# Three more weight slots, two more x tiles turned on the matmul engine, and score banks lent out at the end: a change to a fused attention and gated feed-forward kernel

## The chip, the cores and the metric

The kernel runs on one core of one Trainium2 chip. The metric is the device time of one execution in microseconds (us); the times quoted are medians of several executions. "PE" is the matmul engine (TensorE), "PEld" its weight load, "DVE" the vector engine, "ACT" the scalar engine, "POOL" GpSimd and "SP" the engine that issues most DMAs. Each execution also reports the span from its first to its last instruction and the mean clock that the throttle granted PE, as a share of full speed.

A ratio between two kernels is the mean time of one kernel's runs over the mean of the other's of the same rounds, so it is not quite the ratio of the medians beside it. Intervals are 95%.

## The reference, cut to what matters

```python
def _A_ref(x, wq, wk, wv, wo):            # x: (1, 2048, 1024), bf16
    q = (x @ wq).reshape(B, S, 32, 32).transpose(0, 2, 1, 3)     # 32 heads of 32
    k, v = x @ wk, x @ wv                                        # one key and value head for all
    p = softmax(einsum("bhqd,bkd->bhqk", q, k) * 32 ** -0.5)
    o = einsum("bhqk,bkd->bhqd", p, v)
    return o.transpose(0, 2, 1, 3).reshape(B, S, 1024) @ wo
def _B_ref(x, w_gate, w_up, w_down):      # 1024 -> 3584 -> 1024
    return (sigmoid(x @ w_gate) * (x @ w_up)) @ w_down

h  = x + _A_ref(_layernorm(x), wq, wk, wv, wo)
h2 = h + _B_ref(_layernorm(h), w_gate, w_up, w_down)
```

## The kernel before

The 2048 rows are 16 tiles of 128. Scores are made in 512 "visits": a visit is 8 matmuls with 32-row tiles and 2 exponentials of 1024 columns on ACT. Between the visits PE does everything else: turning x, queries, keys and values, P times V (PV), the O projection (OP), gate and up (GU) and down (D).

The order of all this is not written by hand. The kernel holds a **planner**: a list scheduler in Python that runs when the kernel is built. It keeps a clock for each engine, gives each operation a modelled duration, and picks PE's next work by priority among what is ready. The order that comes out is fixed; the chip only follows it. 65 tuples (`KNOBS`, one for each 8 visits) set priorities and look-ahead.

```python
NPC = 18            # slots of the weight ring, 256 KB each
NST = 3             # buffers for the gated product, hst
NPT = 2             # x tiles turned on PE; the others by transposing DMAs
...
OT   = SB("OT", [2, NG, P])        # O, transposed, of two row tiles
h_sb = SB("h_sb", [4, D])          # residual rows of four tiles
hst  = SB("hst", [NST, FW])
tnh  = SB("tnh", [2, 512], F32)    # tanh of the gate, two buffers
...
S_ps = EC(nc.psum_tensor("S_ps", [P, 6, 512], F32))   # six banks for scores
F_ps = EC(nc.psum_tensor("F_ps", [P, 2, 512], F32))   # two banks for everything else
```

How weights come in: gate and up are 56 pieces of 256 KB for a row tile, in blocks of eight (four gate, four up). Even tiles use the blocks forward and odd tiles backward, so that the blocks at the turn are still in the ring.

```python
def refill():
    m = used[0]
    while True:
        while m < len(USES) and USES[m] in held:      # the next use that isn't held
            m += 1
        ...
        if free_slots:
            sl = free_slots.popleft()
        elif held:
            far = max(held, key=next_use)             # evict what is used farthest away,
            if next_use(far) <= m:                    # unless it is used sooner than the new one
                return
            sl = held.pop(far)
        ...
        held[USES[m]] = sl
        load_piece(USES[m], sl)
```

How PE's next work is chosen, and where fillers (matmuls whose result nobody reads) come from:

```python
PRIO = [["xT", "H", "KV", "Q0", "OP"] + r for r in (["GU", "D", "Q"], ["D", "GU", "Q"])]
...
if v < NV:                          # v: the visit, NV = 512
    ...                             # a score visit, if its banks are free and ACT will run dry
...
banks = [b for b in range(2) if known(bank_rel[b], t)]
for cl in PRIO[KNOBS[v // WIN][2]]: ...               # else the first class that is ready
...
if v and spare:                     # nothing is ready: a filler
    pl.op("pe", mm(F_ps[:, spare[0], 0:256], ident[:, :], kT4[:, 0:256], True, True), ...)
    continue
pl.free["pe"] = t + 50.0            # or PE idles for 50 ns
```

The softmax here doesn't subtract the row's maximum and nothing guards it: scores larger than these inputs give would overflow.

Of the kernel before, what the change touches and what calls it, by code (L numbers as in the profile page):

```python
# [13 lines left out]
P = 128  # L14
# [122 lines left out]
def bass_sequential_preLN__grouped_kv_mqa__glu_gated_glu__prompt_kernel(  # L137
# [33 lines left out]
    KNOBS = [(4, 7, 0, 2, 1, 0, 1), (1, 7, 1, 2, 1, 0, 0), (3, 4, 0, 2, 3, 2, 1), (2, 0, 0, 2, 2, 2, 0), (1, 7, 0, 2, 3, 0, 1), (2, 7, 0, 2, 3, 0, 0), (0, 0, 1, 2, 2, 0, 1), (0, 0, 0, 1, 2, 0, 1), (1, 0, 0, 1, 2, 0, 0), (3, 4, 0, 1, 2, 2, 0), (3, 7, 1, 1, 2, 0, 1), (4, 0, 0, 4, 2, 2, 0), (3, 7, 0, 1, 3, 0, 0), (2, 0, 1, 4, 2, 1, 0), (3, 4, 0, 1, 2, 0, 0), (0, 4, 0, 0, 2, 0, 0), (3, 7, 0, 0, 3, 0, 1), (3, 7, 0, 2, 3, 0, 0), (0, 7, 0, 2, 3, 0, 0), (3, 5, 1, 0, 2, 0, 0), (1, 6, 0, 0, 3, 0, 0), (0, 0, 1, 1, 3, 0, 1), (1, 7, 0, 1, 3, 1, 1), (4, 6, 0, 1, 3, 0, 0), (4, 4, 1, 0, 3, 0, 0), (4, 7, 1, 1, 3, 0, 1), (2, 7, 0, 2, 2, 0, 0), (0, 5, 0, 2, 2, 0, 1), (0, 7, 1, 1, 2, 0, 1), (4, 0, 0, 4, 3, 0, 1), (0, 5, 0, 2, 3, 0, 0), (2, 0, 1, 1, 3, 1, 0), (4, 0, 0, 2, 3, 1, 0), (1, 4, 0, 1, 3, 0, 0), (3, 7, 0, 2, 2, 0, 1), (2, 4, 0, 4, 3, 0, 0), (4, 7, 0, 4, 3, 1, 0), (3, 7, 0, 2, 3, 0, 1), (3, 7, 0, 2, 2, 0, 0), (4, 0, 0, 0, 2, 0, 0), (4, 0, 1, 4, 2, 0, 0), (4, 6, 0, 2, 3, 1, 0), (1, 0, 0, 0, 2, 1, 0), (1, 7, 1, 4, 2, 1, 1), (2, 0, 0, 2, 2, 0, 1), (3, 5, 0, 0, 3, 0, 1), (1, 0, 0, 1, 2, 0, 0), (2, 5, 0, 1, 3, 0, 0), (4, 0, 0, 1, 2, 2, 1), (4, 6, 0, 2, 3, 0, 1), (2, 6, 0, 1, 2, 2, 1), (3, 0, 1, 1, 2, 2, 0), (0, 0, 1, 4, 2, 0, 0), (4, 6, 1, 1, 3, 1, 0), (0, 0, 0, 2, 3, 2, 0), (0, 7, 1, 1, 2, 0, 0), (4, 4, 0, 1, 2, 0, 1), (1, 0, 0, 4, 3, 2, 1), (4, 0, 0, 0, 2, 1, 1), (4, 5, 1, 4, 2, 0, 0), (1, 0, 0, 4, 3, 2, 0), (2, 6, 0, 2, 1, 2, 0), (4, 0, 0, 2, 2, 0, 1), (4, 4, 0, 2, 2, 0, 0), (4, 0, 0, 2, 2, 0, 0)]  # L171
# [3 lines left out]
    NPC = 18  # L175
    NST = 3
# [7 lines left out]
    with ExitStack() as es:  # L184
# [16 lines left out]
        OT = SB("OT", [2, NG, P])  # L201
        h_sb = SB("h_sb", [4, D])
# [4 lines left out]
        tnh = SB("tnh", [2, 512], F32)  # L207
# [36 lines left out]
        OcX = h_sb[:, :, :].rearrange("p a b -> p (a b)").bitcast(F32).rearrange("p (a b) -> p a b", a=NX)  # L244
# [48 lines left out]
        c_w = pl.op("dve", lambda: DVE.memset(hact[:, 0:512], 0.0), occ=150)  # L293
# [5 lines left out]
        def load_x(ts, deps=()):  # L299
            sl = slice(ts[0] * P, (ts[-1] + 1) * P)  # L300
            o = dma(lambda: SP.dma_start(x_sb[:, ts[0]:ts[-1] + 1, :], xf[sl, :].rearrange("(a p) n -> p a n", p=P)),
                    f"x{ts[0]}", P * D * 2 * len(ts), deps, prio=1 if ts[0] > 5 else 0)
            for t in ts:
                x_ld[t] = o

        def load_wq(a, b, deps=()):
            o = dma(lambda: SP.dma_start(wq2[a // 4][:, :, a % 4 * P:(a % 4 + b - a) * P], A_wq[:, a * P:b * P].rearrange("(a p) n -> p a n", p=P)),
                    f"wq{a}", D * P * (b - a) * 2, deps, prio=0)
            for g in range(a, b):
                wq_ld[g] = o  # L310

        wk_ld = pl.op("act", lambda: ACT.dma_start(wk_sb, A_wk.rearrange("(a p) j -> p a j", p=P)), prio=0, key="wk",
                      occ=450.0, lat=3700.0)
        wv_ld = pl.op("act", lambda: ACT.dma_start(wv_sb, A_wv.rearrange("(a p) j -> p a j", p=P)), prio=0, key="wv",
                      occ=450.0, lat=6000.0)
        x0_ld = [dma(lambda hf=hf: SP.dma_start(x_sb[:, 0, hf * 512:(hf + 1) * 512], xf[0:P, hf * 512:(hf + 1) * 512]),  # L316
                     f"x0{hf}", P * D, (), prio=0) for hf in range(2)]
        x_ld[0] = x0_ld[1]
# [3 lines left out]
        load_wq(2, 4)  # L322
        load_wq(4, 8)
        load_x([4, 5])
        warm = pl.op("act", lambda: ACT.activation(out=tnh[:, 0, 0:1], in_=half, func=ACTF.Exp), [c0], prio=1, occ=1400)
# [68 lines left out]
        bank_rel = [[], []]  # L394

# [60 lines left out]
        NPT = 2  # L456
# [286 lines left out]

        def mk_PV(G, h):
            qb, g = G // ND, 2 * (G % ND)

            def block(b):
                r, rs = [], []
                k0, k1 = 8 * h, 8 * h + 8
                for kt in range(k0, k1):  # L750
                    kq, kk = kt // KB, kt % KB
                    for j in range(4):
                        slot = slot_of[(G, kq, j // 2)]
                        co = (j % 2) * 512 + kk * 256
                        r.append(mm(F_ps[DH * j:DH * (j + 1), b, 0:256], Vb[:, kt, :], pslot(slot)[:, co:co + 256],
                                    kt == k0, kt == k1 - 1, tile_position=(0, DH * j)))
                        if h == 0 and G < NX:
                            rs.append(mm(F_ps[DH * j:DH * (j + 1), b, 256:512], ones[:, :], pslot(slot)[:, co:co + 256],
                                         kt == k0, kt == k1 - 1, tile_position=(0, DH * j)))
                for j in range(4 if h else 0):  # L760
                    r.append(mm(F_ps[DH * j:DH * (j + 1), b, 256:512], ones[:, :],
# [3 lines left out]
            def after(b, last):  # L765
                pv_done[(G, h)] = last
                free_p_slots(last)
                O, R = F_ps[:, b, 0:256], F_ps[:, b, 256:512]
                if h == 0 and G < NX:
                    oc_ev[G] = pl.op("dve", lambda: DVE.tensor_copy(out=OcX[:, G, :], in_=F_ps[:, b, :]), [last],  # L770
# [10 lines left out]
                Ob = OcX[:, G, 0:256] if G < NX else Oc[:, :]  # L781
# [3 lines left out]
                if G < NX:  # L785
                    c = pl.op("dve", lambda: DVE.tensor_tensor(out=Rc[:, :], in0=R, in1=OcX[:, G, 256:512], op=ALU.add),  # L786
                              [last, oc_ev[G], o_ev.get(G - 1)], prio=0, **t_dve(256))
                    rel.append(c)
                    load_xr(G, rel[:])
                    c = pl.op("dve", lambda: DVE.transpose(out=Rc[:, :], in_=Rc[:, :]), [c], prio=2, **t_dve(256))  # L790
                else:
                    c = pl.op("dve", lambda: DVE.transpose(out=Rc[:, :], in_=R), [last, o_ev.get(G - 1)], prio=0,
                              **t_dve(256))
                    rel.append(c)
                r = pl.op("dve", lambda: DVE.reciprocal(Ri[:, :].unsqueeze(2), Rc[:, :].rearrange("p (a b) -> p a b", b=DH)[:, :, 0:1]),
                          [c], prio=2, occ=109, lat=270)
                d = pl.op("dve", lambda: DVE.transpose(  # L797
                    out=Rc[:, :], in_=Ri[:, :].unsqueeze(2).to_broadcast([P, 2 * P // DH, DH])), [r],
                    prio=2, **t_dve(256))
                o_ev[G] = pl.op("dve", lambda: DVE.tensor_tensor(  # L800
                    out=OT[:, qb % 2, g:g + 2, :], in0=Oc[:, :].rearrange("p (a b) -> p a b", a=2),
                    in1=Rc[:, :].rearrange("p (a b) -> p a b", a=2), op=ALU.mult),
                    [a, d, op_last.get(qb - 2)], prio=2, **t_dve(256))
                if g == NG - 2:
                    for dc in range(2):
                        queues["OP"].append(mk_OP(qb, dc))
# [9 lines left out]
            gr.gate = lambda: qb < 2 or (qb - 2) in op_last  # L816
            return gr

        def emit_PV(t):

            banks = [b for b in range(2) if b not in [cur_b] + [x[2] for x in below] and known(bank_rel[b], t)]
# [23 lines left out]

        def load_xr(t, deps):
            if t < NT:
                xr_ld[t] = dma(lambda: SP.dma_start(h_sb[:, t % 4, :], xf[t * P:(t + 1) * P, :]), f"xr{t % 4}", P * D * 2,
# [4 lines left out]
        def mk_OP(t, dc):  # L853
            def atoms(b):
                return [(mm(F_ps[:, b, :], OT[:, t % 2, g, :],
                            wo_sb[:, g, dc * 512:(dc + 1) * 512], g == 0, g == NG - 1), 512, []) for g in range(NG)]

            def after(b, last):
                sl = slice(dc * 512, (dc + 1) * 512)
                h_ev[(t, dc)] = pl.op("dve", lambda: DVE.tensor_tensor(  # L860
                    out=h_sb[:, t % 4, sl], in0=F_ps[:, b, :], in1=h_sb[:, t % 4, sl], op=ALU.add),
                    [last, xr_ld[t]], prio=1, **t_dve(512))
                if dc == 1:
                    op_last[t] = last
                    sv = stats(1, [t], [h_sb[:, t % 4, :]], [[h_ev[(t, 0)], h_ev[(t, 1)]]], 3)
                    hnorm[t] = norm(1, t, h_sb[:, t % 4, :], hn[:, :], sv, [hT_ev.get(t - 1)], 2)
# [3 lines left out]
            gr = Group("OP", atoms, lambda: [o_ev[t * ND + g] for g in range(ND)] + [xr_ld[t]] + wo_ld, after)  # L870
            gr.gate = lambda: len(wo_ld) == NG and t in xr_ld and (t < 1 or (t - 1) in hT_ev)
# [73 lines left out]
        def mk_GU(i):  # L945
# [9 lines left out]
            def atoms(b):  # L955
                sl = [held[it] for it in its]
                r = []
                for dt in range(DT):
                    d = dt // DPP
                    r.append((mm(F_ps[:, b, :], hnT[:, t % 2, dt, :], piece(sl[d])[:, dt % DPP, :], dt == 0, dt == DT - 1), FW,  # L960
# [8 lines left out]
            def after(b, last):  # L969
# [3 lines left out]
                if w == 0:  # L973
                    tanh_of[n] = pl.op("act", lambda: ACT.activation(  # L974
                        out=tnh[:, n % 2, :], in_=F_ps[:, b, :], func=ACTF.Tanh, scale=0.5),
                        [last, tn_user.get(n % 2)], prio=1, **t_act(FW))
                    return [tanh_of[n]]
                e = pl.op("dve", lambda: DVE.scalar_tensor_tensor(  # L978
                    out=hst[:, n % NST, :], in0=tnh[:, n % 2, :], scalar=1.0, in1=F_ps[:, b, :],
                    op0=ALU.add, op1=ALU.mult), [last, tanh_of[n], st_ev.get(n - NST)], prio=0, **t_dve(FW))  # L980
                tn_user[n % 2] = e
# [15 lines left out]
        def mk_D(t, dc, c0=0, n=512):  # L997
            fts = [4 * p + f for u, p in TP if u == t for f in range(4)]

            def atoms(b):  # L1000
                return [(mm(F_ps[:, b, 0:n], hactT[:, t % 2, ft, :], wd_sb[:, ft, dc * 512 + c0:dc * 512 + c0 + n],
                            ft == fts[0], ft == fts[-1]), n, [hact_ev[(t, ft)]] if dc == 0 else []) for ft in fts]

            def after(b, last):
# [4 lines left out]
                    out=h_sb[:, t % 4, sl], in0=F_ps[:, b, 0:n], scalar=0.5, in1=h_sb[:, t % 4, sl],  # L1009
                    op0=ALU.mult, op1=ALU.add), [last], prio=2 - KNOBS[min(v, NV - 1) // WIN][6], **t_dve(n))  # L1010
                out_dma[(t, dc + c0 / 512)] = dma(lambda: SP.dma_start(of[t * P:(t + 1) * P, sl], h_sb[:, t % 4, sl]),
                                       f"o{t % 4}{dc}{c0 // 256}", P * 2 * n, [e], prio=2)
                if (t, 1 - dc) in out_dma and t + 4 < NT:
                    load_xr(t + 4, [out_dma[(t, 0)], out_dma[(t, 1)]])
# [24 lines left out]
        while True:  # L1039
# [43 lines left out]
            else:  # L1083
                pick = None
                banks = [b for b in range(2) if known(bank_rel[b], t)]
# [27 lines left out]
            if v == 0 and known([c_id, c_w], t):  # L1113
                pl.op("pe", mm(S_ps[:, 5, :], ident[:, :], hact[:, 0:512], True, True), [c_id, c_w],
                      **t_mm(512 if t > 7000.0 else 1024)).tag = "dummy"
# [116 lines left out]
```

## Time and profile before

| | before |
|---|---|
| time, median of 3 | 1080.24 us (1079.57 to 1081.72) |
| span of the profiled run, granted clock | 1077.7 us, 1.000 |
| PE busy | 1067.9 us, 99% |
| ACT busy | 1008.2 us, 94% |
| gate and up pieces loaded | 316 + 316 + 12 + 10 = 654 |

PE is the engine to look at: it is busy for 99% of the span and ACT stops 60 us before the end. Two more views of this kernel matter later. The first is PE's timeline of the head. The columns are start, length, engine, line, operation, output from inputs, count, and in brackets the idle time before it with what ended it.

```profile
15.58 0.40 PE L404 MATMUL S_ps<-QTb,kT 32*128 32x256 bf16 x8
15.91 1.29 PE L404 MATMUL F_ps<-zone 128*128 128x128 bf16 x17
17.39 1.07 PE L404 MATMUL F_ps<-zone 128*128 128x128 bf16 x16 [0.18 <-ACT QTb L285]
18.58 0.40 PE L404 MATMUL S_ps<-QTb,kT 32*128 32x256 bf16 x8
```

`S_ps<-QTb,kT` x8 is one score visit. The second and third visits start 3.0 us apart, and PE fills the time between with projections (`F_ps<-zone`). The other view is the DMA part of the page, with packets, megabytes and the share of the 16 engines' time:

```profile
q1 hardware_dynamic: 308512, 225.51, 80.8%
```

### The profile page before, as it was taken

To read this page: it belongs to the slowest core of one execution; us is meant where nothing else is said; L and a number is where in the kernel's file an instruction comes from. 1 tells how busy PE (TensorE), PEld (TensorE's weight loads), DVE (VectorE), ACT (ScalarE), POOL (GpSimd) and SP (SyncE) were. 2 spreads that over 40 slices of the span, in tenths; PEclk is the share of its full clock that TensorE was granted. 3 is DMA by queue.
4 is the path that set the end of the run, shared out by engine and by line. 5 is a ranking of instruction groups with operands and counts; after the bars stand their busy time and mean duration, and the time that the engine had idled before them with its cause. 6 is when DMAs were issued, how large, how long until landed. Compare 5 with 4: busy or idle time off the path is not lost.

```text
span 1077.7 us, 31536 instructions
## 1 busy us (share of the span) xinstructions
PE 1067.9 (99%) x12961; PEld 486.2 (45%) x12961; DVE 901.5 (84%) x1731; ACT 1008.2 (94%) x1168; POOL 31.7 (3%) x58
## 2 busy tenths in 40 slices
PE   8999999999999999999999999999999999999999
PEld 6754444444444444444444444444444444444445
DVE  7889998888988888898888889898898988898721
ACT  6999999999999999999999999999999999999700
POOL 2100000000000000000000000000000000000000
PEclk9999999999999999999999999999999999999999
DMA  9996998939679595959779495978869496977995
GB/s 242 187 312 207 238 267 235 269 79 277 172 211 240 153 257 128 280 131 254 197 187 270 122 276 120 260 179 220 234 158 250 113 283 144 242 190 187 272 281 126
DMA packets 310735, 227.65 MB, mean 211 GB/s; under 512 B 121920, under 2 KB 302016, under 8 KB 310592
## 3 DMA queue, kind: packets, MB, share of 16 engines
q1 hardware_dynamic: 308512, 225.51, 80.8%
q8 instruction: 102, 1.67, 0.7%
q10 hardware_dynamic: 2080, 0.13, 0.1%
q14 instruction: 41, 0.34, 0.1%
HBM read 195.17 MB, written 7.86 MB: 188 GB/s over the span
## 4 chain that ended last, share of the span: by engine, by line
PE 96%; DVE 1%; ACT 1%; DMA 1%; issue 1%; SPq 0%; DVEq 0%
PE F_ps L404 80%; PE S_ps L404 16%; ACT Pr L696 1%; DMA ring<-in_A_x_dram 1%; DVE Ts L730 0%; DVE Rc L786 0%; ACT QTb L285 0%; DVE hact L286 0%; SPq L316 0%; DVE Rc L797 0%; DVE OT L800 0%; DVE Rc L790 0%; DVE st L339 0%; DVE Ts L737 0%; ACT hact L285 0%
## 5 line engine op out<-in xcount | busy, mean ns | idle before, releaser
L696 ACT ACTIVATE Pr<-S_ps 128x1024 bf16<-128x1024 f32 x1024 | 970.9, 1184 | 2.8 <-PE S_ps L404 2.4
L730 DVE TENSOR_TENSOR Ts<-Ts,Pr 128x1024 bf16<-128x1024 bf16 x736 | 482.0, 676 | 33.8 <-ACT Pr L696 31.6
L404 PE MATMUL F_ps<-ring,hnT 128*128 128x512 bf16 (+1 forms) x2096 | 431.4, 380 | 2.2 <-issue 1.6
L404 PEld LDWEIGHTS F_ps<-ring,hnT 128*128 128x128 bf16 (+1 forms) x2096 | 154.9, 97 | 194.5 <-issue 50.1
L404 PE MATMUL F_ps<-zone,hact 128*128 128x512 bf16 (+2 forms) x1215 | 223.0, 375 | 0.2 <-issue 0.2
L404 PE MATMUL S_ps<-QTb,kT 32*128 32x256 bf16 x4096 | 210.0, 273 | 0.3
L404 PEld LDWEIGHTS S_ps<-QTb,kT 32*128 32x128 bf16 x4096 | 65.5, 92 | 208.2 <-ACT Pr L696 141.5
L404 PE MATMUL F_ps<-Pr,Vb 128*32 128x256 bf16 x4096 | 135.3, 274 | 0.0
L404 PEld LDWEIGHTS F_ps<-zone,hact 128*128 128x128 bf16 (+1 forms) x1215 | 83.7, 97 | 90.5 <-issue 20.9
L974 ACT ACTIVATE tnh<-F_ps 128x512 f32<-128x512 f32 x112 | 84.5, 755 | 41.6 <-PE F_ps L404 41.6
L730 DVE TENSOR_TENSOR Ts<-Pr 128x1024 bf16<-128x1024 bf16 x128 | 86.8, 684 | 36.7 <-ACT Pr L696 36.3
L978 DVE SCALAR_TENSOR_TENSOR hst<-tnh,F_ps 128x512 bf16<-128x512 f32 x112 | 76.5, 683 | 46.5 <-PE F_ps L404 44.5
L404 PEld LDWEIGHTS F_ps<-Pr,Vb 128*32 128x32 bf16 x4096 | 97.6, 96 | 30.2 <-issue 15.0
L404 PE MATMUL F_ps<-zone 128*128 128x256 bf16 (+4 forms) x640 | 74.1, 269 | 1.4 <-DVE Rc L786 1.1
L404 PE MATMUL F_ps<-wo_sb,OT 128*128 128x512 bf16 (+1 forms) x313 | 64.5, 380 | 0.0
L404 PEld LDWEIGHTS F_ps<-zone 128*128 128x128 bf16 (+1 forms) x640 | 43.4, 97 | 23.5 <-issue 7.2
L737 DVE TENSOR_TENSOR Ts<-Ts 128x1024 bf16<-128x1024 bf16 x64 | 44.0, 687 | 1.4
L1008 DVE SCALAR_TENSOR_TENSOR h_sb<-F_ps,h_sb 128x512 bf16<-128x512 f32 (+1 forms) x33 | 22.2, 671 | 22.7 <-PE F_ps L404 22.4
L351 POOL TENSOR_SCALAR zb<-mvb 128x1 bf16<-128x1 bf16 (+1 forms) x25 | 10.7, 426 | 993.0 <-DVE mvb L343 993.0
L404 PEld LDWEIGHTS F_ps<-wo_sb,OT 128*128 128x128 bf16 (+1 forms) x313 | 22.4, 97 | 28.1 <-issue 6.8
L782 DVE TENSOR_TENSOR Oc<-F_ps,Oc 128x256 f32<-128x256 f32 x60 | 25.3, 422 | 4.8 <-PE F_ps L404 3.1
L286 DVE COPY Oc<-F_ps 128x256 f32<-128x256 f32 x60 | 25.2, 420 | 4.8 <-PE F_ps L404 4.0
(60 smaller groups left out, 323.8 us busy)
## 6 DMA issues: line engine op xcount, KB each, us to landing
ring<-in_B_w_gate_dram SPq DMA_DIRECT2D x316, 256.0 KB, 4.4
ring<-in_B_w_up_dram SPq DMA_DIRECT2D x316, 256.0 KB, 4.6
zone<-in_B_w_down_dram SPq DMA_DIRECT2D x28, 256.0 KB, 3.9
h_sb<-in_A_x_dram SPq DMA_DIRECT2D x16, 256.0 KB, 4.3
out_dram<-h_sb SPq DMA_DIRECT2D x31, 128.0 KB, 2.9
ring<-in_A_x_dram SPq DMA_DIRECT2D x7, 512.0 KB, 6.6
QTb<-q_scratch SPq DMA_DIRECT2D x14, 256.0 KB, 4.8
Pr<-in_B_w_gate_dram SPq DMA_DIRECT2D x12, 256.0 KB, 4.6
```

What stands on the lines that cost most here:

```text
L286: lambda: DVE.tensor_copy(out=out_ap, in_=in_ap))
L351: f = pl.op("pool", lambda: POOL.tensor_scalar(out=zb[:, ph, sl].unsqueeze(2), in0=mvb[:, ph, sl, 1:2], scalar1=LN_EPS_BF16, scalar2=None, ...
L404: fn = lambda: PE.matmul(o, lhsT=l, rhs=r, start=start, stop=stop, **kw)
L696: exps[u] = pl.op("act", lambda slot=slot, pb=pb: ACT.activation(out=pslot(slot).rearrange("p (a b) -> p a b", a=2), in_=S_ps[:, pb:pb + 2 ...
L730: o = pl.op("dve", lambda T=T, a=a, b=b: DVE.tensor_tensor(out=T, in0=a, in1=b, op=ALU.add), deps, prio=4, **t_dve(1024, 1.92))
L737: merge_ev[G] = pl.op("dve", lambda T4=T4: DVE.tensor_tensor(out=T4[:, :, 0, :], in0=T4[:, :, 0, :], in1=T4[:, :, 1, :], op=ALU.add), [sum ...
L782: a = pl.op("dve", lambda: DVE.tensor_tensor(out=Oc[:, :], in0=O, in1=Ob, op=ALU.add), [last, oc_ev[G], o_ev.get(G - 1)], prio=0, **t_dve( ...
L974: tanh_of[n] = pl.op("act", lambda: ACT.activation(out=tnh[:, n % 2, :], in_=F_ps[:, b, :], func=ACTF.Tanh, scale=0.5), [last, tn_user.get ...
L978: e = pl.op("dve", lambda: DVE.scalar_tensor_tensor(out=hst[:, n % NST, :], in0=tnh[:, n % 2, :], scalar=1.0, in1=F_ps[:, b, :], op0=ALU.a ...
L1008: e = pl.op("dve", lambda: DVE.scalar_tensor_tensor(out=h_sb[:, t % 4, sl], in0=F_ps[:, b, 0:n], scalar=0.5, in1=h_sb[:, t % 4, sl], op0=A ...
```

## The change: intent and diff

Four buffers become smaller, and the space goes to three more weight slots, to save weight loads. At the head x tiles 2 and 3 are turned on PE, x tile 0 comes over two queues and the fillers are narrower. At the end the six score banks serve any group once the scores are over, and the last O projection is split. All 65 tuples are new, so the whole order is another one.

```diff
-    NPC = 18
-    NST = 3
+    NPC = 21
+    NST = 2
+    NH = 3
...
-        OT = SB("OT", [2, NG, P])
-        h_sb = SB("h_sb", [4, D])
+        OT = SB("OT", [NG, P])
+        h_sb = SB("h_sb", [NH, D])
-        tnh = SB("tnh", [2, 512], F32)
+        tnh = SB("tnh", [512], F32)
...   # head
+        x0_ld = [dma(x_half(0, SP), "x00", P * D, prio=0),
+                 pl.op("act", x_half(1, ACT), prio=0, key="x01", occ=450.0, lat=2800.0)]
...
-        NPT = 2
+        NPT = 4
...
-            if v == 0 and known([c_id, c_w], t):
-                pl.op("pe", mm(S_ps[:, 5, :], ident[:, :], hact[:, 0:512], True, True), [c_id, c_w], ...)
+            if v == 0 and known([c_w], t):
+                pl.op("pe", mm(S_ps[:, 5, 0:P], hact[:, 0:P], hact[:, 0:P], True, True), [c_w], ...)
...   # end
+        def FB(b):
+            return F_ps[:, b, :] if b < 2 else S_ps[:, b - 2, :]
...
+                if v == NV and len(bank_rel) == 2:
+                    bank_rel.extend([exps[u] for u in range(2 * NV - 3, 2 * NV) if u % NB == k // 2] for k in range(6))
...
-            pl.free["pe"] = t + 50.0
+            pl.free["pe"] = t + 20.0
...   # KNOBS: all 65 tuples replaced; F_ps[:, b, ...] becomes FB(b)[...] throughout
```

The value weights also move to SP behind part of the query weights, and an eighth field of the tuples can let the norm after the O projection go ahead of other work.

## The prediction

> **What bounds the kernel now.** I read the page first (busy shares, chain), then the chain in order of time near the end, the timeline of the first 25 us and of the tail, the list of waits, and the groups by form.
>
> The page says who is full and who set the end:
>
> ```profile
> PE 1067.9 (99%) x12961; PEld 486.2 (45%) x12961; DVE 901.5 (84%) x1731; ACT 1008.2 (94%) x1168; POOL 31.7 (3%) x58
> ...
> PE 96%; DVE 1%; ACT 1%; DMA 1%; issue 1%; SPq 0%; DVEq 0%
> ```
>
> ACT is nearly full too, but only until its last exponential at about 1015 us; PE then goes on alone for 60 us with gate, up and down matmuls. PE can do that work at any time, so the end is PE's start plus PE's total work plus PE's holes. A busy PE need not be a PE at its peak, so I checked its pace. From the chain in order of time (start us, length us, what, instructions):
>
> ```profile
> 1002.88 0.33 PE S_ps L404 x8
> 1003.21 1.40 PE F_ps L404 x6
> ...
> 1010.47 2.05 PE F_ps L404 x9
> ...
> 1012.85 6.40 PE F_ps L404 x132
> 1019.25 0.29 issue
> 1019.54 55.63 PE F_ps L404 x311
> ```
>
> Three more matmuls of 512 columns cost 2.05 - 1.40 = 0.65 us, 0.216 us each. Then 1.40 - 6 x 0.216 = 0.10 us of that piece is no column work[...]. A score piece is two quads of 256 columns, 2 x 0.109 = 0.22 us[...]. Every one of the 512 score visits pays about 0.21 us.
>
> Summing PE's work from the groups by form: gate and up 1632 + 44 full and 116 quads (464 / 4), down 771 + 97 and 55 half-width, O 237 + 19, queries 121 + 7: some 3072 matmuls of 512 columns x 0.216 = 663 us; 248 of 256 columns x 0.109 = 27; 160 of 128 columns x 0.056 = 9; values 128 x 0.025 = 3; scores, PV and sums (4096 + 4096 + 256 + 128) / 4 = 2144 quads x 0.109 = 234; [...]. Together 1044 us. The first useful matmul starts at 7.06 us, and 2.5 us follow the last. That makes 1053; the span is 1077.7. So **only some 25 us at most** is neither fixed work nor the two ends, and that includes what the sum misses (a few ns per visit). Two per cent of the time is 21.6 us.
>
> The head shows holes (timeline: start, length, what, idle before it):
>
> ```profile
> 1.67 4.96 PE L404 MATMUL S_ps<-hact,ident 128*128 128x512 bf16 x12 [1.67 <-POOL ident L290]
> ...
> 4.09 0.69 DVE L341 BATCH_NORM_STATS2 st<-ring 128x6 f32<-128x512 bf16 x1 [0.26 <-DMA ring<-in_A_x_dram]
> ...
> 7.06 0.66 PE L433 MATMUL F_ps<-ident,ring 128*128 128x128 bf16 x8 [0.43 <-DVE ring L385]
> ...
> 9.76 0.38 PE L404 MATMUL S_ps<-hact,ident 128*128 128x512 bf16 x1
> 10.73 0.62 PE L433 MATMUL S_ps<-ident,ring 128*128 128x128 bf16 x8 [0.59 <-DVE ring L388]
> ...
> 21.30 0.83 PE L404 MATMUL F_ps<-kT,ident 128*128 128x256 bf16 x6 [0.43 <-ACT QTb L285]
> ```
>
> Matmuls on ident with hact or kT are fillers whose result nobody uses: 18 and 11 in the whole run. At 21.3 us PE ran dry for about 1.1 us (0.43 idle, 6 x 0.11 filler) before the keys and values of x tiles 2 and 3, whose DMA transposes were issued at 14.8 us.
>
> [...]
>
> **The change, part by part.**
>
> 1. *Head.* The halves of x tile 0 go out on two queues, the value weights later. Their statistics now start at 3.14 and 4.09 us; the second would follow at once, 3.83: 0.26 us earlier. One issue fewer (0.43 us) precedes x tile 1, which is wanted at about 5.9. Estimate: 0.5 us on the path to the first score. Narrower fillers cannot hold PE for 0.43 us when data arrive: at most 0.3 us at the two places above. The second-queue half puts the key weights about 0.5 us later; they landed at 3.6 and are used at 8.2, so this is free.
>
> 2. *x tiles 2 and 3 on PE.* Adds 16 transposes at about 0.056 us back to back (128 columns, as the 8 at 7.06), 0.9 us of PE, and 4 evacuations of 0.54 us on ACT (two took 1.09), 2.2 us in a stretch where ACT idles about 3 us anyway (none of its exponentials start between 21.0 and 24.5). Takes away the 1.1 us hole. Net on PE about -0.2 us; ACT should reach the fourth exponential pair some 3 us sooner, which by itself moves no end.
>
> 3. *18 to 21 weight slots.* 316 + 316 + 12 + 10 = 654 pieces are loaded for 16 x 56 = 896 uses, so 242 were found in place, 16 at each of 15 turns. Three slots more save at most 45 loads of 256 KB, 12 of 227.65 MB, 5%. But in the whole list of waits no row has PE or its weight load waiting for a DMA: the saved transfers were hidden. About 0, perhaps 0.5 us of odd fillers (five after 100 us).
>
> 4. *The smaller buffers.* tanh: in the tail, the tightest place, tanh starts at 1040.59 and 1044.04 us, and the product reading the first runs 1042.32 to 1043.01: one buffer still leaves 1.0 us. hst: two products later is 1049.22, while the transposing DMA issued at 1043.37 with the 4.5 us median lands near 1047.9: 1.3 us left. Residual: tile 15's slot now waits for tile 12's down result (945 us) instead of tile 11's; its use is at 1023. O: tile 14's O matmuls end near 965 and tile 15's first O is written at 975. All four fit; cost 0, with hst the thinnest.
>
> 5. *Score banks at the end, O of the last tile split, faster last norm.* After 1019.54 the chain is 55.63 us of PE without a hole: 8 matmuls every 1.73 us. Before it stands one 0.29 us "issue" and a wait of similar size. Down matmuls of tile 14 (1026.6 to 1038.7) already cover the last norm and its transpose, issued at 1029.35. So more banks remove at most 0.5 us.
>
> 6. *A new order of everything else.* The 65 tuples are new. They can only remove holes: my estimate of the scattered ones between 50 and 1015 us is under 10 us, the rest of the 25 being the head and what my sum misses. I give 1 us.
>
> Sum: -0.8 (1) -0.2 (2) -0.3 (3) +0 (4) -0.5 (5) -1.0 (6) = -2.8 us, 1080.2 to **1077.4 us**.
>
> **Rivals.** (a) *A weight-bound kernel*: if slots were scarce, the schedule might have dodged missing weights in ways no wait shows, and 45 loads fewer would be worth 5 to 10 us: about 1071. For it: DMA queues busy 80.8%; against it: eleven kT fillers in all. (b) *A new wait from the thin buffers*: [...]112 products with a loss of 0.05 to 0.1 us would cost 5 to 10 us: about 1084. For it: the issue of two such transposes took 4.64 us at 1060; against it: outside the tail pairs lie much further apart than 3.45 us. (c) *ACT sets the end*: ACT runs exponentials without a break, so 2.2 us more on it might come out whole: about 1079. Against it: 60 us of PE work remain when ACT stops. (d) *A shorter dependency tail* worth many microseconds: about 1065, only if PE were waiting there, and it is not.
>
> **Range and chances.** The fixed 1053 plus the 2.5 us between span (1077.7) and time (1080.2) makes 1056 a floor that the change cannot come near; most of (a) would give 1071, most of (b) 1083. I take 1071 to 1082 for 8 in 10. Faster by over 2% needs 1058.6, nearly the floor: 0.01. Slower by over 2% needs 1102, 22 us of new waits in a schedule made for these buffers: 0.02.
>
> **What would show it.** (1) The first transposes of x near 6.8 us and first scores near 12.7 instead of 13.4. (2) No fillers near 21 us, 16 more transposes, exponentials without a 3 us break there. (3) Near 610 weight pieces, less DMA share, still no PE wait for DMA. (4) No new DVE wait before the products on hst. (5) A tail after the last score as long as now (about 65 us), other banks or not. (6) PE 99% busy again. I am wrong if PE's tail shrinks by many microseconds with the same work in it, or if PE waits on DMA or DVE where it did not.

The term 512 x 0.21 = 108 us went with them. "Together 1044 us" was worked out with that term; the terms left standing come to 936. The 0.21 us is 0.10 as above and 0.33 - 0.22 = 0.11. The trace of the kernel before shows such a time, though not its cause: the first score matmul starts 0.312 us (median) after a 512-column matmul on the full array, where a second one of those starts after 0.216; and the first 512-column matmul on the full array starts 0.200 us after the last of the visit's score matmuls, whose two groups of four start 0.109 us apart. That is 0.096 and 0.091, 0.19 us for a visit. No part of the diff takes out a visit. The 0.43 us of a wide filler in part 1 is the 0.427 us at which the first of them follow each other, up to 5.91 us; from 7.55 us on they do so every 0.216.

## The result, and the profile after

| | before | after |
|---|---|---|
| time, median of 4 runs each | 1080.02 us (1079.57 to 1081.72) | 1080.68 us (1079.85 to 1081.98) |
| ratio | | 1.0004 [0.9987, 1.0022] |
| span of the profiled run, granted clock | 1077.7 us, 1.000 | 1079.0 us, 0.998 |
| last matmul starts | 1074.88 us | 1076.22 us |
| gate and up pieces loaded | 654 | 318 + 316 + 10 + 10 = 654 |

The time did not move. The busy shares and the chain that ended last, on the page of the changed kernel:

```profile
PE 1069.8 (99%) x13080; PEld 490.4 (45%) x13080; DVE 902.3 (84%) x1735; ACT 1009.7 (94%) x1168; POOL 30.7 (3%) x58
...
PE 88%; ACT 10%; issue 1%; DMA 1%; DVE 1%; SPq 0%
```

PE is still 99% busy. The chain now takes a detour over ACT's exponentials around 762 to 865 us, where ACT is busy for all of the 103 us and PE fills the time between visits; the last 60 us of it are PE alone, as before. PE's instruction count grows by more than the 16 transposes: there are more and narrower fillers, and more of the full-array matmuls are issued as four narrow ones.

**The head.** The same stretch of PE's timeline as shown of before:

```profile
14.62 0.40 PE L414 MATMUL S_ps<-QTb,kT 32*128 32x256 bf16 x8
...
15.40 0.40 PE L443 MATMUL F_ps<-ident,ring 128*128 128x128 bf16 x4
16.59 0.89 PE L443 MATMUL F_ps<-ident,ring 128*128 128x128 bf16 x8 [0.80 <-ACT QTb L289]
18.49 0.40 PE L443 MATMUL F_ps<-ident,ring 128*128 128x128 bf16 x4 [1.01 <-ACT zone L289]
18.98 3.07 PE L414 MATMUL F_ps<-zone 128*128 128x128 bf16 x23
21.98 0.61 PE L414 MATMUL S_ps<-QTb,kT 32*128 32x256 bf16 x8
```

The second visit is at 14.62 instead of 15.58, about 1 us earlier. Then come the 16 new transposes (`F_ps<-ident,ring`) in three parts with 0.80 and 1.01 us of idleness between them: each part needs a bank that ACT has to empty first. The queries for the third visit stand behind them, so that visit starts at 21.98 instead of 18.58. What ACT does meanwhile:

```profile
16.38 0.65 ACT L289 ACTIVATE zone<-F_ps 128x512 bf16<-128x512 bf16 x1
16.86 1.08 ACT L706 ACTIVATE Pr<-S_ps 128x1024 bf16<-128x1024 f32 x1
17.76 1.76 ACT L289 ACTIVATE zone<-F_ps 128x512 bf16<-128x512 bf16 x3
```

An exponential (`Pr<-S_ps`, 1.08 us) stands ahead of three of the four evacuations (`zone<-F_ps`). PE's first wait (0.80 us) ended with a query evacuation (`QTb`), its second (1.01 us) with one of those three. Then the 23 matmuls that follow take 3.07 us. By the planned order they are 16 of 128 and 7 of 256 columns, which at the durations of the kernel before is 16 x 0.056 + 7 x 0.109 = 1.66 us; in the trace of experiment 3 below, at full clock, the same 23 take 1.83 us. The array runs at half speed here for most of them: the granted clock is 0.50 from 19.36 us on. The view by windows has a stretch, PE busy (instructions), PEld, DVE, ACT, POOL, the granted clock, the DMA share and GB/s:

```profile
15.40:18.50 3.10, 1.20 (x14) 0.69 (x14) 2.46 (x5) 3.10 (x6) 0.00 (x0) 1.00 0.93 311
18.50:20.30 1.80, 1.71 (x20) 1.53 (x21) 1.80 (x6) 1.02 (x2) 0.85 (x2) 0.74 0.25 90
20.30:22.40 2.10, 2.10 (x18) 1.07 (x15) 1.96 (x7) 0.38 (x1) 0.10 (x1) 0.50 0.00 0
```

PE was busy for 1.20 of the 3.10 us of this stretch, and after that the clock falls to 0.50. The clock records put the half-speed stretch at 19.36 to 22.77 us, 3.413 us long, the only one inside the run. The clock changes in this trace at 5.71, 19.36, 22.77 and, after the last instruction, 1080.90 us. These changes lie 13.653, 3.413 and 1058.132 us apart, to about 0.1 us 4, 1 and 310 times 3.413; in the trace of the kernel before there are two, at 6.15 and 1077.94 us, 314 times 3.413 apart. The stretches of 3.413 us counted off from such a change are called windows below. (15.40 to 18.50 us is not one of them; those come under experiment 1.)

**The weights.** The changed kernel's DMA rows, to set beside the 316 + 316 + 12 + 10 of before (count, KB each, us to landing):

```profile
ring<-in_B_w_gate_dram SPq DMA_DIRECT2D x318, 256.0 KB, 4.7
ring<-in_B_w_up_dram SPq DMA_DIRECT2D x316, 256.0 KB, 4.6
...
Pr<-in_B_w_gate_dram SPq DMA_DIRECT2D x10, 256.0 KB, 4.2
Pr<-in_B_w_up_dram SPq DMA_DIRECT2D x10, 256.0 KB, 4.6
```

654 again, not one fewer. The queue moved 224.92 MB against 225.51, at a share of 82.2% against 80.8%.

**In the middle** there is a stall that the kernel before has not, at 769 to 773 us. `F_ps<-kT,ident` are fillers:

```profile
769.12 0.27 PE L414 MATMUL F_ps<-kT,ident 128*128 128x256 bf16 x1
...
770.79 0.94 PE L414 MATMUL F_ps<-kT,ident 128*128 128x256 bf16 x7
...
772.02 1.16 PE L414 MATMUL F_ps<-kT,ident 128*128 128x256 bf16 x9
```

These fillers were in the plan: the planner held back the next gate and up group because it reckoned that a weight piece would land only at 771.5 us. They are baked into the order, whatever the chip does.

**The end.** The chain in order of time (start, length, what, instructions):

```profile
1014.77 1.64 PE F_ps L414 x44
1016.41 5.52 PE S_ps L414 x107
1021.93 1.83 PE F_ps L414 x20
1023.76 4.32 PE S_ps L414 x20
```

`S_ps` here are score banks lent to other groups, and the holes near 1019 us are gone. But from the last score visit to the end of the span it is 1079.0 - 1014.38 = 64.6 us, against 1077.7 - 1012.45 = 65.2.

**What the planner expected.** By its own clock, PE's last matmul would end 1.2 us earlier than in the kernel before (1074.6 against 1075.8 us). From 50 to 1010 us the trace of the kernel before is 0.1 to 0.7 us behind the plan. Two things differ more. In the changed kernel the chip falls from 0.3 us behind the plan at 15 us to 1.6 behind at 51, and stays there (0.2 behind at 50 us in experiment 3, which keeps its full clock): the plan knows no half-speed window. And the tail of the kernel before is shorter than planned. From the last score matmul to the last matmul the planner, run without a chip, has 63.5 us for the kernel before and 61.7 for the changed one; the traces have 62.3 and 61.7 (61.9 in experiment 3). So of the 1.8 us by which the planner found the new tail shorter, the chip shows 0.4 to 0.6. At the last score the plan itself has the changed kernel 0.6 us behind.

**Where the time went.** I summed PE's useful column work (without transposes and fillers) up to several points of both traces. How far the changed kernel is ahead of (+) or behind (-) the kernel before, in us of work; the third column is the kernel of experiment 3 below, which never throttles:

| up to | after | 16 fillers | what lies before it |
|---|---|---|---|
| 50 us | -3.0 | -1.8 | the head |
| 765 us | -0.1 | +0.8 | the steady part |
| 780 us | -2.3 | -1.3 | the planned stall |
| 1000 us | -1.7 | -0.4 | the steady part |
| last matmul, later by | 1.3 | 0.2 | the tail |

The new order does win in these traces: 2.9 us (or 2.6) between 50 and 765 us, some 1 us after 780. The head and the stall take it back. Each column is one traced run, and runs of one kernel differ by 1 us and more, so the tenths are not to be trusted.

### The profile page after: what moved, and what is told of

It is laid out like the page before. It is cut to its first block, busy times and chain, and to the rows that moved or that the text cites. A ratio compares the mean times of both kernels' runs of the same rounds, so it can differ in the third digit from the quotient of the medians.

```text
span 1079.0 us, 31597 instructions
## 1 busy us (share of the span) xinstructions
PE 1069.8 (99%) x13080; PEld 490.4 (45%) x13080; DVE 902.3 (84%) x1735; ACT 1009.7 (94%) x1168; POOL 30.7 (3%) x58
## 3 DMA queue, kind: packets, MB, share of 16 engines
q1 hardware_dynamic: 307296, 224.92, 82.2%
## 4 chain that ended last, share of the span: by engine, by line
PE 88%; ACT 10%; issue 1%; DMA 1%; DVE 1%; SPq 0%
PE F_ps L414 69%; PE S_ps L414 18%; ACT Pr L706 9%; ACT tnh L1008 1%; DMA ring<-in_B_w_up_dram 0%; DMA ring<-in_A_x_dram 0%; DVE Rc L805 0%; ACT zone L289 0%; DVE Ts L740 0%; DVE st L345 0%; ACT QTb L289 0%; PE F_ps L443 0%; DVE st L347 0%; DVE ring L383 0%; PE S_ps L443 0%
## 5 line engine op out<-in xcount | busy, mean ns | idle before, releaser
L414 PE MATMUL F_ps<-ring,hnT 128*128 128x512 bf16 (+1 forms) x1957 | 417.0, 380 | 1.7 <-issue 0.7
L414 PEld LDWEIGHTS F_ps<-ring,hnT 128*128 128x128 bf16 (+1 forms) x1957 | 147.7, 97 | 187.8 <-issue 48.5
L414 PE MATMUL F_ps<-zone,hact 128*128 128x512 bf16 (+2 forms) x1164 | 209.4, 377 | 0.7 <-issue 0.7
L414 PE MATMUL S_ps<-QTb,kT 32*128 32x256 bf16 x4096 | 207.2, 273 | 0.1
L414 PEld LDWEIGHTS F_ps<-zone,hact 128*128 128x128 bf16 (+1 forms) x1164 | 75.0, 97 | 83.5 <-issue 23.0
L1012 DVE SCALAR_TENSOR_TENSOR hst<-tnh,F_ps 128x512 bf16<-128x512 f32 x107 | 73.2, 684 | 38.4 <-PE F_ps L414 36.8
L1008 ACT ACTIVATE tnh<-F_ps 128x512 f32<-128x512 f32 x105 | 78.5, 747 | 5.7 <-PE F_ps L414 5.7
L414 PE MATMUL F_ps<-wo_sb,OT 128*128 128x512 bf16 (+1 forms) x294 | 60.9, 380 | 0.2 <-issue 0.2
L1008 ACT ACTIVATE tnh<-S_ps 128x512 f32<-128x512 f32 x7 | 4.2, 597 | 35.3 <-PE S_ps L414 35.3
```

What stands on the lines that cost most here:

```text
L414: fn = lambda: PE.matmul(o, lhsT=l, rhs=r, start=start, stop=stop, **kw)
L1008: tanh_of[n] = pl.op("act", lambda: ACT.activation(out=tnh[:, :], in_=FB(b), func=ACTF.Tanh, scale=0.5), [last, tn_user.get(0)] + (tn_more ...
L1012: e = pl.op("dve", lambda: DVE.scalar_tensor_tensor(out=hst[:, n % NST, :], in0=tnh[:, :], scalar=1.0, in1=FB(b), op0=ALU.add, op1=ALU.mul ...
```

## The experiments

Two theories stood at the start. **Theory A**: the change is worth a few us, as predicted, and the half-speed window in the head eats them. **Theory B**: the parts are worth nothing by themselves, and what the time depends on is how well the tuples fit the exact setting. Runs 1 to 3 test A, the others test B and the single parts.

### 1. The changed kernel again

No edit.

> The changed kernel once more, as the partner of the next run. Both theories: 1079.9 to 1082.0 us, and again one half-rate window of 3.41 us near 19 to 23 us in the profile (mean granted clock 0.998). If the window is an accident of this one profile, the clock is 1.000 here and the theory of a throttled head falls.

Measured: 1079.89 us (1079.80 to 1081.62, 5 runs), ratio 1.0000 [0.9987, 1.0012]. The profiled run shows the half-speed window again, at 19.22 to 22.63 us. But the runs are of two kinds. Their granted clocks tell which: two at 0.998, three at 1.000. One window of 3.41 us at half speed lowers the mean over 1079 us by 0.5 x 3.41 / 1079 = 0.0016, so a run at 0.998 is one with the window. Counted over every run of a kernel with this head, also of experiments 4, 5 and 9:

| kernel | runs at 0.998 | mean, us | runs at 1.000 | mean, us | difference |
|---|---|---|---|---|---|
| changed, first set | 2 | 1081.64 | 2 | 1079.96 | 1.7 |
| changed, second set (1) | 2 | 1081.33 | 3 | 1079.85 | 1.5 |
| 18 slots (4) | 2 | 1088.18 | 2 | 1086.84 | 1.3 |
| shorter prefetch (5) | 2 | 1098.29 | 2 | 1096.79 | 1.5 |
| no lent banks (9) | 2 | 1081.70 | 2 | 1080.55 | 1.2 |

Ten of 21 runs throttle, and they take 1.2 to 1.7 us longer than the others of their kernel, without overlap in any of the five rows: the loss in the head isn't made up later. None of the 38 runs of the kernel before that stood beside the experiments throttles. Why it is about half of them I can only estimate. Each trace has its own window boundaries, counted off in steps of 3.413 us from its changes of clock. In the three traced runs that throttled, the window just before the half speed (15.94 to 19.36, 15.81 to 19.22, 16.08 to 19.50 us) held only 1.57, 1.42 and 1.80 us of busy PE. In the two that did not, the boundaries lay at 16.72 and 20.14, and at 17.27 and 20.69, and these windows held 2.22 and 2.21 us. The estimate from these numbers assumes a limit on PE's busy time in the window, which no run shows: let the limit lie anywhere between 1.80 and 2.21 us, and slide a window over PE's busy times in the trace of experiment 9. It falls below the limit for 40 to 64% of all positions of the boundaries; 10 of 21 is 48%.

### 2. 52 fillers in the idle time of the head

```diff
+            if v == 2 and known([exps[1], k_ev[0]], t):
+                enter("full")
+                pl.op("pe", mm(S_ps[:, 2, 0:P], ident[:, :], kT4[:, 0:P], True, True), [k_ev[0], exps[1]], **t_mm(P)).tag = "dummy"
+                continue
```

> Only filler matmuls are added in the idle stretches of PE between the second and third score visit (15.6 to 18.5 us); every other instruction keeps its order. Theory 'throttled head' (PE too idle there, so its clock is halved for one 3.41 us window and 1.7 us of column work is lost): clock 1.000, third score visit at about 20.5 us instead of 21.98, and the whole span about 1.4 us shorter (1077.6). Rival 'the evacuations of the turned tiles on ACT are the whole loss': the third visit stays within 0.3 us of 21.98 and the span within 0.4 us.

Measured: 1081.40 us (1081.33 to 1082.35, 5 runs), ratio 1.0012 [0.9999, 1.0024]. All five runs have a clock of 1.000 and the third visit comes at 20.87 us. PE is busy for all of the 3.10 us from 15.40 to 18.50 us instead of for 1.20, and no run throttles: that bears out a PE too idle in the head as the cause. The gain did not come: a miss. The trace shows where its lead over the throttled run went. It is 1.16 us at the 61st visit and 0.27 at the 81st. Between them:

```profile
141.68 1.10 PE L414 MATMUL F_ps<-ring,hnT 128*128 128x512 bf16 x3 [1.01 <-DMA ring<-in_B_w_up_dram]
```

PE, being early, waits for an up weight. From 125 to 150 us the DMA share is 1.14 (the summed times of the packets, which pass 1 here), but it is 1.17 in experiment 3, which waits only 0.2 us, so full queues alone don't make the wait. What differs is the start of the weight stream: 57.60 us in this traced run, 56.12 in experiment 3.

### 3. 16 fillers instead of 52

One every 0.18 us; every other instruction on every engine stands as in the changed kernel.

```diff
+        fill_t = [0.0]
...
-            if v == 2 and known([exps[1], k_ev[0]], t):
+            if v == 2 and known([exps[1], k_ev[0]], t) and t >= fill_t[0]:
+                fill_t[0] = t + 180.0
```

> The changed kernel with 16 filler matmuls of 128 columns (one every 0.18 us) in the idle stretch of the head instead of the 52 of the earlier filler run; every other instruction stands in the changed kernel's order. So far 10 of 21 runs with the unmended head show a mean clock of 0.998 and take 1.2 to 1.7 us more than the others of the same kernel (changed kernel in its two sets: 1081.3, 1082.0, 1081.6, 1081.0 against 1079.8 to 1080.1), and none of 15 with the 52 fillers, but those without re-fitted knobs took 1081.3 to 1082.4, 1.5 us more than the unthrottled runs of the changed kernel. Theory 1 (activity decides, fillers are free): array busy 2.0 of the 3.1 us, no run at 0.998, third score visit near 20.8 us, all runs near the unthrottled 1079.9, ratio near 0.9995. Theory 2 (16 are too few): some runs at 0.998, and those 1.5 us longer. Theory 3 (arriving earlier only meets the weights near 141 us, where the queues are full): clock 1.000 in all, and again 1081.3 or so, with a wait of PE for an up weight of about 1 us near 141 us and the lead over the throttled trace (1.2 us at visit 60) gone by visit 80.

Measured: 1079.91 us (1079.80 to 1080.24, 5 runs), ratio 0.9998 [0.9984, 1.0012], all five at 1.000. The same windows as above, in this kernel:

```profile
15.40:18.50 3.10, 1.98 (x28) 1.40 (x25) 1.70 (x3) 3.10 (x7) 0.00 (x0) 1.00 0.96 320
18.50:20.30 1.80, 1.73 (x26) 1.54 (x27) 1.80 (x6) 1.24 (x4) 0.17 (x1) 1.00 0.32 118
20.30:22.40 2.10, 2.10 (x44) 1.64 (x42) 2.10 (x7) 1.38 (x3) 0.78 (x2) 1.00 0.00 0
```

The third visit, at full clock:

```profile
19.06 1.83 PE L414 MATMUL F_ps<-zone 128*128 128x128 bf16 x23
20.83 0.40 PE L414 MATMUL S_ps<-QTb,kT 32*128 32x256 bf16 x8
```

1.98 us busy of 3.10 instead of 1.20 is enough in these five runs, and 44 matmuls instead of 18 go through in 20.3 to 22.4 us. In this trace no window of 3.413 us around the thin stretch, wherever its boundaries lie, holds less than 2.22 us of busy PE. Theory 1 of this run holds: five runs near the unthrottled 1079.9. It also bounds Theory A. Without the window the changed kernel is level with the kernel before, not 2.8 us faster; the window costs some 1.4 us in half of the runs, 0.7 on average. This trace waits only 0.2 us for weights near 139 us. Why the kernel with 52 fillers is 1.4 us slower in each of its five runs stays open: one of the five was traced, and the late weight stream in that one fits. The stream begins at 57.60, 57.12 and 57.63 us in the three traces with 52 fillers (experiments 2, 10 and 12), and at 56.12, 56.12 and 56.56 in the unthrottled traces with 16 or none (3, 9 and 5). That speaks for the fillers; by what way they would delay the stream is not shown.

### 4. 18 slots in the changed kernel

```diff
-    NPC = 21
+    NPC = 18
```

> The changed kernel with 18 weight slots instead of 21, all else and all knobs kept. Prediction's view (slots are hidden, no fewer loads matter): at most 1 us slower, about 1081.5. Rival (what counts is how far ahead the weights can be fetched, and the knobs are fitted to that): the kernel's own planner, which follows the chip's trace within half a us per stretch, puts its end 10 us later, so about 1090, with more PE holes before gate and up matmuls.

Measured: 1087.39 us (1086.82 to 1088.43), ratio 1.0064 [1.0049, 1.0079], with 644 pieces loaded. Going back to 18 slots costs 7 us. That looks as if the three slots were worth 7 us; experiments 8 and 10 show that it can't be read so.

### 5. Shorter prefetch

```diff
+                if m >= used[0] + 16:
+                    return
```

> 21 slots, but a piece is fetched only within 16 uses of its own, so that used pieces stay longer: 565 weight loads instead of 654, 23 MB less traffic. If traffic bounds anything: faster, or at least not slower. If the depth of the prefetch counts and traffic does not: slower by up to 20 us (planner: PE end 1094.9), although 14% fewer weights are moved.

Measured: 1097.63 us (1096.36 to 1098.54), ratio 1.0158 [1.0144, 1.0172]. The traffic did fall, to 565 pieces:

```profile
DMA packets 284413, 203.78 MB, mean 186 GB/s; under 512 B 118384, under 2 KB 275696, under 8 KB 284272
```

Less traffic and a slower kernel: the bytes are not what holds it. The trace has 106 `kT` fillers instead of 22, each put where the planner found nothing ready, which speaks for pieces that come late. Because the tuples were not fitted to this setting either, the size of the loss is not the price of the prefetch alone.

### 6. The smaller buffers alone, in the kernel before

```diff
-    NST = 3
+    NST = 2
+    NH = 3
-        OT = SB("OT", [2, NG, P])
+        OT = SB("OT", [NG, P])
...   # h_sb and tnh as in the change; 18 slots, the old head, end and tuples
```

> The kernel before with the smaller buffers alone (3 residual, 1 tanh, 1 O, 2 hst buffers), 18 slots, its own knobs and head. PE, ACT and DVE keep every instruction in the same order. Prediction's view: no wait follows, same within 0.5 us (1080.0). Rival 'thin buffers': DVE or ACT wait for the transposes or the tanh buffer, 5 to 10 us slower.

Measured: 1080.45 us (1079.24 to 1082.46), ratio 1.0003 [0.9990, 1.0015]. PE, ACT and DVE even keep the very order of the kernel before. The four buffers fit. One wait is new in the traces of this run and the next: in the tail PE waits 0.7 and 0.4 us for the landing of a transpose of `hst`, the buffer that the prediction called the thinnest. The trace of the kernel before has no such wait; whether the smaller buffers cause it is not shown.

### 7. Smaller buffers and lent banks

Experiment 6 with the change's end: `bank_rel` extended, the last O projection split.

> The same with the end banks as well (score banks lent out after the last score, O of the last tile in two parts); the order changes only after 1000 us. Prediction's view: at most 0.5 us faster than the run with the buffers alone, since PE had no hole there. Rival 'the tail waits for banks': several us faster.

Measured: 1081.34 us (1080.19 to 1082.60), ratio 1.0009 [0.9995, 1.0022]: nothing that can be told from zero.

### 8. Smaller buffers and 21 slots, with the tuples of before

Experiment 6 with `NPC = 21`.

> The kernel before with the smaller buffers and 21 slots, its own knobs kept. Taking 3 slots from the changed kernel cost 7 us. Theory 'depth is worth 7 us': giving 3 slots to the kernel before makes it faster. Theory 'the knobs are fitted to one exact setting, any departure costs 5 to 10 us, and the slots as such little': this one is slower too, by 5 to 10 us (about 1087), with as many weight loads as before, about 650.

Measured: 1088.87 us (1087.49 to 1092.18), ratio 1.0082 [1.0065, 1.0100], with 656 pieces loaded. **Three slots more** with the tuples of 18 slots cost 9 us; three slots fewer with the tuples of 21 slots cost 7 (experiment 4). So a slot count for which the tuples were not fitted costs several us by itself, and experiment 4 doesn't give the price of slots. The loss shows in the tail. In all 14 traces the last score visit starts between 1012.0 and 1014.9 us; from there to the last matmul it takes 62 to 63 us in those near 1080 us, and 66 to 79 in the slower ones (experiments 4, 5, 8, 10 and 11): less of PE's other work was done between the visits. One of the four runs of this experiment had a clock of 0.998 with the old head; it was not the traced one, so where it throttled is not known.

### 9. The changed kernel without the lent banks

```diff
-                if v == NV and len(bank_rel) == 2:
-                    bank_rel.extend(...)
...   # and the last O projection whole again
```

> The changed kernel without the end banks (score banks not lent out, O of the last tile in one part); the order is the same up to the last score. Prediction's view: the end banks are worth at most 0.5 us, so 1080 to 1081 us, the same as the changed kernel. Rival 'the tail needs the banks': 2 us or more slower.

Measured: 1081.20 us (1080.28 to 1081.81), ratio 0.9999 [0.9985, 1.0014] to the kernel before on the same chip, which took 1080.97 there. With experiment 7 the end shows no worth from either side; each interval reaches some 1.5 us either way, so half a us can't be excluded.

### 10. 18 slots with tuples searched anew

Experiment 4 with the 52 fillers, and the tuples searched by some 1,700 random trials of the planner, by its own clock.

> The changed kernel with the head fillers and 18 slots again (which cost 7 us with the knobs kept), but with its knobs searched anew for 18 slots by 1,700 tries of the kernel's own planner. Theory 'misfit of the knobs': most of the 7 us comes back, about 1083 to 1084, and more searching would bring more. Theory 'depth of the ring': it stays near 1087.

Measured: 1083.31 us (1082.66 to 1085.15), ratio 1.0024 [1.0006, 1.0042]. In the planner's clock the search took PE's end from 1084.9 to 1077.6 us. On the chip some 4 of the 7 us of experiment 4 came back with the 18 slots kept, give or take 2.5. So probably more than half of those 7 us was the fit (the fillers differ too). Whether a longer search would find the rest isn't settled.

### 11. The old head in the changed kernel

`NPT = 2`, x tile 0 over one queue, the wide fillers, the new tuples kept. A first build was found to write into a bank whose sum was still open; the bank is now held from the start of the split projection.

> The changed kernel with the old head (x tiles 2, 3 turned by DMA, x tile 0 on one queue, wide fillers); knobs kept, so its later part is not fitted. Theory 'throttled head': no half-rate window, third score visit near 18.6 us instead of 22, and last DMA transpose of x issued about 47.5 us, 2 us sooner than with the new head. In total slower all the same by some 4 us for the knobs. If the clock is halved here too, the turned tiles are not its cause.

Measured: 1083.91 us (1083.65 to 1085.02), ratio 1.0031 [1.0016, 1.0047]. The third visit came at 18.35 us with a clock of 1.000, so the old head reaches the third visit sooner; yet the kernel is 3 us slower. The likely reason is that the tuples were searched for what follows the other head. Undoing one part of a planned kernel does not measure that part.

### 12. 21 slots, 52 fillers, tuples searched anew

The same search, with the same number of trials.

> The changed kernel with the head fillers and 21 slots, knobs searched anew with the same number of tries (the planner gains 0.9 us by it). Expected clock 1.000, scores at the 60th visit about 1 us before the changed kernel's. Theory 'the first filling of the weights is bound by DMA near 140 us': that lead is gone again by the 80th visit, with PE waiting for a weight piece between, and the total is within 1 us of the kernel before (1079 to 1081). Rival: the wait of the earlier run was an accident, the lead stays, and the total is 1078 to 1079.

Measured: 1079.79 us (1078.91 to 1080.29, 6 runs), ratio 0.9986 [0.9975, 0.9998] to the kernel before (1080.97, 11 runs). All at 1.000; the last matmul starts at 1073.87 us, 1.0 us earlier than in the kernel before. This is the only version ahead of the kernel before beyond its interval, and only by 0.14%: weak evidence, since it is one of twelve comparisons, the traced run is the fastest of its six, and the kernel before scattered from 1079.44 to 1083.51 us on this chip, all at full clock, for no reason that a run shows. Its trace has the wait for an up weight near 141 us too (0.98 us), so the search gained elsewhere.

Set beside experiment 10 (same chip and rounds, same fillers, same search), 21 slots are 3.5 us faster than 18. How much of that is the slots and how much the luck of the search isn't settled: the kernel before reaches 1080 us with 18 slots.

## Why the prediction was right or wrong

The class (within 2%) and the range were right, and so was the reason: PE's own work fills the time and nothing in the diff removes any. The predicted 1077.4 us was 3.3 too low. Some of the agreement is luck: a range of 11 us is wide beside a change of 3, and a gain that was larger than expected covered most of a loss that wasn't foreseen. By its own steps:

- **Step 1, head, -0.8 us with the narrower fillers: right in sign, lost at once.** The first visit starts at 12.68 instead of 13.42 us. But traces of kernels with the old head scatter from 12.80 to 13.57, and with the new one from 12.54 to 13.20, so how much of that 0.7 is the change's can't be told.
- **Step 2, x tiles 2 and 3, -0.2 us: this is the step that failed.** I had counted PE's 0.9 us of transposes and a hole of 1.1 us that goes away, and put the four evacuations "in a stretch where ACT idles about 3 us anyway". That stretch was 21.0 to 24.5 us in the kernel before; the transposes were placed at 15.4 to 18.9, where ACT is busy for all of 3.10 us. So PE waited 0.80 and 1.01 us for evacuations, and the third visit, behind them, moved from 18.58 to 20.83 us even unthrottled (experiment 3). The thin stretch then switched the array to half speed in 10 of 21 runs, which I had not considered at all. Steps 1 and 2 together: -1.0 predicted; in work done by 50 us, 1.8 us behind without the window and 3.0 with it. The exponentials "without a 3 us break" are wrong too: ACT's next exponential after 16.86 starts at 22.64 in the changed kernel.
- **Step 3, slots, -0.3 us: wrong in the count, the worth not shown.** "At most 45 loads" less became none. The blocks of eight share one order, and the rule fetches whatever is used next as soon as something farther can go. Replayed without a chip, the rule keeps 16 pieces over each turn for any ring from 16 to 23 slots, which the chip's 654 and 654 bear out for 18 and 21 (the replay has 656; buffers of the scores that serve as slots at the end save a few); a third block needs 24. "Near 610 weight pieces" and "less DMA share" were therefore wrong. PE's weight waits were nearly none, as said, with small new ones (0.2 to 1.0 us near 140 us); but the stall at 769 to 773 us is a weight wait that the planner covered with fillers, so PE's list of waits doesn't show it. That was rival (a)'s argument, though not at its size. What three slots are worth once the tuples fit no run tells: experiments 10 and 12 differ by 3.5 us.
- **Step 4, buffers, 0: right within noise.** Experiment 6: 1.0003, the order unchanged, with a new wait of 0.7 us in its trace's tail.
- **Step 5, the end, -0.5 us: neither shown nor refuted.** The holes near 1019 us are gone, the tail is 64.6 instead of 65.2 us, and experiments 7 and 9 give 1.0009 and 0.9999 with and without.
- **Step 6, a new order, -1.0 us: sum about right, made of larger terms.** In the unthrottled trace 2.6 and 1.1 us are won on either side of the planned stall, with the tail in the second figure, and 2.1 are lost in it: 1.6 us won. I had not expected a stall to be written into the order, nor that most of what the planner saw in the new order was a tail that the chip ran faster than the plan in the kernel before.

The sum without the window: -1.8 (head) + 2.6 - 2.1 + 1.1 = -0.2 us of work, so 0.2 us later where -2.8 was predicted. 2.8 of these 3.0 us are in steps 1 and 2. Of the rivals, none came at its size: no weights-bound gain, no loss from thin buffers, and the tail hardly shrank. Theory A of the experiments is right for 0.7 us on average and no more. Theory B is right and larger: keeping the tuples while a slot count changes costs 7 to 9 us (experiments 4 and 8), more than any part of the change.

## What to carry to other kernels

A kernel whose order was searched must not be taken apart piece by piece: fit it again after each edit, or compare only stretches in which the order is the same. Before work is moved to an engine, look at what the other engine that must empty its banks does **at that moment**, not some us later, and keep the matmul array busy over such a gap; with 16 narrow fillers none of 5 runs throttled here, against 10 of 21 without, and three times as many were no better. To count what a larger cache saves, run its replacement rule: here slots that don't complete a block save no loads. And compare a plan with the trace part by part before its gains are believed: the planner's 1.8 us in the tail were 0.4 to 0.6 on the chip.

## What the traces show of the clock, the transposes and the changes of tile

- After three windows of 3.413 us with PE busy for 1.42 to 1.80 us the clock was 0.50 for one window; after the thinnest windows of 2.21 and 2.22 us in two unthrottled traces it was not. No idle gap in them was longer than 1.01 us. Without the transposes the busy times are 0.21 to 0.61 us against 1.08 and 1.19, so no run here tells whether the transposes count. The throttling came in 10 of 21 runs with the new head, each 1.2 to 1.7 us longer; with 16 fillers (at least 2.22 us in any window) it came in none of 5.
- A transpose of 128x128 takes 222 ns in the mean (24 of them in the changed kernel), and back to back they overlap: four take 0.40 us and eight 0.66, about 0.06 us for each further one.
- A change of PE between the full array, 32-row tiles and 32-column tiles costs 0.09 to 0.11 us. In the trace of the kernel before the matmuls start 0.312 us apart at the change from full-array ones of 512 columns to the scores and 0.200 at the change back, against 0.216 and 0.109 without a change, and there are some 1,000 changes. What PE does in that time is not shown.
